# Block 0 of an attention and SwiGLU kernel: a root for each half on GpSimd, masks of the first weight pieces on VectorE, the silu table loaded first, and a written order

## The chip, the cores and the metric

The kernel runs on one core of a Trainium2 chip. The core has TensorE (matrix products and transposes, into PSUM), VectorE, ScalarE and GpSimd for elementwise work, and SyncE, which here issues nearly all DMA transfers. The engines run in parallel; each takes its own instructions in order, and semaphores make one wait for another. The metric is the device time of one execution in microseconds. A difference of 0.2% is taken here as the least that counts.

## The reference

```python
kv = np.einsum('bhsd,bhse->bhde', k, v)
out = np.einsum('bhsd,bhde->bhse', q, kv)
rms = np.sqrt(np.mean(out * out, axis=-1, keepdims=True) + 1e-06)
return (out / rms * g_norm).astype(np.float32)
...
x = np.ascontiguousarray(attn_out.transpose(0, 2, 1, 3)).reshape(B * S, H * D)
g = x @ w_gate
silu = g * (1.0 / (1.0 + np.exp(-g)))
val = x @ w_val
return (silu * val @ w_out).astype(np.float32)
```

B = 8 batches, H = 8 heads, S = 576 positions, D = 64. The 4608 tokens have 512 features; the hidden width is 1536. The inputs q, k, v and g_norm are fp32; the three weight matrices come to the chip as 64-bit words.

## The kernel before

**Tiling.** The 4608 tokens are nine blocks of 512. `Att` makes the normalised attention output x of a block, transposed so that features lie on partitions; `Ffn` multiplies it with the weights. Blocks 1 to 8 use Strassen's scheme, one or two levels deep (`Quad`, `Up`, `Inner`, `Down`, lines 544 to 940). Block 0 uses plain products (`plain_up`, lines 1026 to 1041) for the first layer, since its weights are still being prepared, and `Down` for the second.

**Weights.** Each word's high half holds the sign, the exponent and the upper bits, the low half the rest. `Words` (lines 119 to 167) turns one piece of 128x512 into fp32. `begin` takes the magnitude of the high half (ScalarE, Abs, line 146), clamps it (VectorE, line 147), masks the sign (VectorE, line 152), shifts and joins the two (VectorE, line 153). `finish` scales the low half to a unit (ScalarE, line 160) and adds it (VectorE, line 162). There are 36 pieces: w_gate and w_val in turn, 24 of them, and then 12 of w_out. `weights(n)` (line 1063) rounds pieces up to n, and keeps loading four pieces ahead (line 135, 512 KB each, on SyncE). The landing tiles come from a pool of four (`ld`), shared with k, v and q: a transfer waits until the tile's last reader is done.

**Block 0's start.** `first` (line 466): `turn_q` transposes q tiles on TensorE and copies them out of PSUM (lines 337 to 341), `first_kv` makes k'v for half of the heads (line 248), `heads` multiplies q with it (line 361). `squares` squares the products on ScalarE (line 374) and sums each head's 64 squares on VectorE (line 375). `root` takes the inverse root of both halves (256 tokens each) at once: scaling by 1/64 plus eps (line 381), a first guess by integer arithmetic (line 384), three Newton steps of three operations (lines 391 to 393), all on VectorE with tiles of 128x32. `scale` multiplies the products by it (line 113, a helper), two operations for each half; `turn_x` transposes the result on TensorE (line 410) and copies it with the gain to x on ScalarE (line 411). `warm` (line 492) runs seven products of 512 columns whose result nobody reads. Then `plain_up` (lines 1035 to 1041) multiplies x with w_gate and w_val for one of twelve slices of the hidden width, applies silu on ScalarE (line 1040) and multiplies on VectorE (line 113); slice 0 is done in halves of the tokens.

**What sets the order.** The framework orders each engine's instructions by a simulation of its own. `tc.issue_after(ins)` puts what the block traces behind `ins`, for those of its instructions that run on the engine of `ins`; it adds no wait between engines. In block 0 such lines put piece 0's `begin` behind the first half's sums and q's last copy, the second half's products behind piece 0, and the rounding of later pieces behind copies of `turn_x` (line 1094: for slice 0 behind those of the first half, from slice 1 on behind those of the second).

**Where block 0 meets block 1.** Block 1's k, v and q are loaded on SyncE behind the last weight pieces (lines 1102 to 1106). q comes in 32 small transfers (line 284) into two `ld` tiles; VectorE transposes each tile (line 331). TensorE's order in `down` (line 1002) is one product of block 0's second layer, then both halves of block 1's `heads`, then the other products.

Of the kernel before, what the change touches and what calls it, by code (L numbers as in the profile page):

```python
# [1 line left out]

# [16 lines left out]
def kernel(  # L19
# [41 lines left out]
    nc = tc.nc  # L61

    B, H, S, D = q.shape
# [7 lines left out]
    NS = DM // P  # L71
# [4 lines left out]
    eps = 1e-6  # L76
# [6 lines left out]
    consts = pool("consts", 1)  # L83
    ld_pool = pool("ld", 4)
    st_pool = pool("st", 2)
# [26 lines left out]
    sub = lambda e, o, a, b: e.tensor_tensor(out=o, in0=a, in1=b, op=OP.subtract)  # L112
    mul = lambda e, o, a, b: e.tensor_tensor(out=o, in0=a, in1=b, op=OP.mult)  # L113

    def ring():

        return r_pool.tile([P, 4, BLK], F32, name="r")

    class Words:
# [12 lines left out]
        def __init__(self, src, shape):  # L132
            self.raw = ld_pool.tile([P, LD], U32, name="ld")[:, 0 : 2 * BLK]
            dst = self.raw.rearrange("p (a b) -> p a b", a=shape[0])
            self.sent = nc.sync.dma_start(out=dst, in_=src)
            self.shape = shape
            self.begun = False

        def begin(self):

            self.begun = True
            halves = self.raw.rearrange("p (f w) -> p f w", w=2)
            low, high = halves[:, :, 0], halves[:, :, 1]
            self.low, self.room = low, ring()
            mag = self.mag = self.room[:, 1].bitcast(U32)
            nc.scalar.activation(out=mag.bitcast(F32), in_=high.bitcast(F32), func=ACT.Abs)
            nc.vector.tensor_scalar(
                out=mag.bitcast(F32), in0=mag.bitcast(F32), scalar1=self.LOW, scalar2=self.HIGH,
                op0=OP.max, op1=OP.min,
            )  # L150
            sign = self.room[:, 2].bitcast(U32)
            nc.vector.tensor_scalar(out=sign, in0=high, scalar1=0x80000000, scalar2=None, op0=OP.bitwise_and)
            return nc.vector.scalar_tensor_tensor(
                out=mag, in0=mag, scalar=3, in1=sign, op0=OP.logical_shift_left, op1=OP.bitwise_xor
            )

        def finish(self, dst):

            unit = self.room[:, 0]
            nc.scalar.activation(out=unit, in_=self.low, func=ACT.Copy, scale=2.0**-51, bias=2.0)  # L160
            a, b = self.shape[0], BLK // self.shape[0]
            return nc.vector.tensor_tensor(
                out=dst.bitcast(U32),
                in0=self.mag.rearrange("p (a b) -> p a b", a=a, b=b),
                in1=unit.bitcast(U32).rearrange("p (a b) -> p a b", a=a, b=b),
                op=OP.add,
            )
# [6 lines left out]
    words = {}  # L174
# [18 lines left out]
    class Att:  # L193
# [128 lines left out]
                for r in range(2):  # L322
                    nc.scalar.copy(out=dst[:, r], in_=self.kv_ps[r])

        def turn_q(self, i, pools=None):

            if i == 0:
                self.qt = ring().rearrange("p j (t c) -> p t j c", t=T)
            if self.quarters:
                to = self.qt[:, :, 2 * i : 2 * i + 2].rearrange("p t j c -> p j t c")  # L330
                self.q_turned = nc.vector.transpose(out=to.rearrange("p j t c -> p (j t c)"), in_=self.q[i])
                return
            for t in (2 * i, 2 * i + 1):
                pool = pools[t % 2] if pools else m_psum
                ps = pool.tile([P, NS, P], F32, name=pool.name[0])
                for j in range(NS):
                    nc.tensor.transpose(ps[:, j], self.q[t][:, j], ident)
                if t % 2 if self.n == 0 else t:
                    self.copied_q = nc.scalar.copy(out=self.qt[:, t], in_=ps)
                else:  # L340
                    nc.vector.tensor_copy(out=self.qt[:, t], in_=ps)
# [124 lines left out]
        def first(self):  # L466
            self.turn_q(0, (b_psum, c_psum))
            self.first_kv(0, (b_psum, c_psum))
            last = self.first_kv(1, (b_psum, a_psum))

            with tc.issue_after(last.ins):
                self.heads(0, (0, 1), (m_psum, m_psum))
            with tc.issue_after(self.multiplied.ins):
                self.heads(0, (2, 3))
            self.squares(0)
            with tc.issue_after(self.multiplied.ins):
                self.turn_q(1, (b_psum, c_psum))

            with tc.issue_after(self.copied_q.ins), tc.issue_after(self.summed.ins):
                begun = words[pieces[0]].begin()  # L480
            with tc.issue_after(begun.ins):
                self.product(1, (b_psum, a_psum))
            self.warm()
            self.root(0, 2)
            self.scale(0)
            with tc.issue_after(self.squared.ins), tc.issue_after(self.scaled.ins):
                weights(1)
            self.turn_x(0)
            self.scale(1)
            return self.squared, self.scaled  # L490

        def warm(self):

            ps = c_psum.tile([P, NS, P], F32, name="c")
            for _ in range(7):
                nc.tensor.matmul(ps, lhsT=ident, rhs=self.qt[:, 3], start=True, stop=True)

        def turn(self):
# [443 lines left out]
    class Ffn:  # L942
# [83 lines left out]
        def plain_up(self, f, halves=(0, 1)):  # L1026

            if 0 in halves:
                self.ps[f] = [pool.tile([P, 2, HB], F32, name=pool.name[0]) for pool in (b_psum, c_psum)]
            of = slice(halves[0], halves[-1] + 1)  # L1030
            ps = [t[:, of] for t in self.ps[f]]
            x = self.att.x[:, 0:4].rearrange("p (h m) i t -> p (m i) h t", h=2)
            for t, w in zip(ps, (wg, wv)):
                for i in range(NS):
                    nc.tensor.matmul(  # L1035
                        t, lhsT=w[f // 2][:, i, P * (f % 2) : P * (f % 2 + 1)], rhs=x[:, i, of],
                        start=(i == 0), stop=(i == NS - 1),
                    )
            h = self.h[:, f].rearrange("p (h t) -> p h t", h=2)[:, of]
            nc.scalar.activation(out=h, in_=ps[0], func=ACT.Silu)  # L1040
            mul(nc.vector, h, h, ps[1])
# [37 lines left out]
    blocks[0].load_q(1)  # L1079
    load_weights(4)  # L1080
    squared, scaled = blocks[0].first()

    for n in range(NB):
        ffn = Ffn(n, blocks[n])
        nxt = blocks[n + 1] if n + 1 < NB else None
        if n == 0:

            with tc.issue_after(squared.ins), tc.issue_after(scaled.ins):
                weights(2)
            ffn.plain_up(0, (0,))  # L1090
            copied = blocks[0].copied
            blocks[0].turn_x(1)
            for f in range(NF):
                with tc.issue_after(blocks[0].copied.ins if f else copied.ins):
                    weights(2 * (f + 2))
# [12 lines left out]
            for g in range(2):  # L1108
                nxt.kv(g)
        else:  # L1110

            def visit(g):
                with tc.issue_after(ffn.multiplied.ins):
                    nxt.kv(g)
                if nxt.n < B:
                    ffn.visited = nxt.positions

            def third():
                visit(0)
# [12 lines left out]
            ffn.up(fill)  # L1132
# [48 lines left out]
```

## Time and profile before

| | us |
|---|---|
| median of 4 runs | 1021.96 (1021.7 to 1022.2) |
| the profiled execution | 1021.87 |
| its span in the profile | 1020.0 |
| TensorE busy in the span | 1002.8 (98%) |
| VectorE busy | 702.1 (69%) |
| ScalarE busy | 228.2 (22%) |
| GpSimd busy | 370.4 (36%) |
| first x in block 0 (turn_x of the first half starts) | at 28.28 |
| from here TensorE multiplies without a wait until block 0's second layer | at 34.83 |
| last product of the plain first layer starts | at 110.49 |
| block 1's second q tile lands | at 121.02 |

Times in the profile count from the start of the span; the run's time is 1.87 us longer than the span. PE is TensorE, PEld its weight load, DVE VectorE, ACT ScalarE, POOL GpSimd, SP SyncE; a q behind the name is the engine's sequencer. In a timeline, the first number is the start, the second the duration, then come engine, line, operation, output and inputs, and the idle time before with what ended it. fp32 products show twice the number of instructions that the code has. The granted TensorE clock is 1.0 throughout.

### The profile page before, as it was taken

The numbers are of one execution on the slowest core, as the hardware profiler recorded it, in microseconds if no ns is written. First come the engines' busy times: TensorE is split into PE (matmuls) and PEld (weight loads), VectorE is DVE, ScalarE is ACT, GpSimd is POOL, SyncE is SP. The second block draws the span as 40 slices with busy tenths as digits, with TensorE's granted clock in tenths as the row PEclk, the third lists the DMA queues.
The fourth block names the chain that finished last, engine by engine and source line by source line (L and its number), as shares of the span: only waits on it lengthen the run. The fifth ranks groups of instructions, "written<-read, shape, count | busy, mean of one in ns | idle before, by whom it ended". The sixth has DMA issues, their size and how long they took to land.

```text
span 1020.0 us, 21397 instructions
## 1 busy us (share of the span) xinstructions
PE 1002.8 (98%) x8522; PEld 895.4 (88%) x8522; DVE 702.1 (69%) x1169; ACT 228.2 (22%) x353; POOL 370.4 (36%) x280
## 2 busy tenths in 40 slices
PE   5999999999999999999999999999999999999998
PEld 4544688888999999998999899988998999989997
DVE  2998788998666946685558576665669466946661
ACT  2765111221211221121121211111121211221110
POOL 0000363434055513561246315630555045513670
PEclk9999999999999999999999999999999999999999
DMA  8689643667888277846685568646872766066601
GB/s 225 198 265 258 129 92 110 183 160 163 253 221 252 53 187 204 245 89 139 207 238 135 100 208 241 170 62 193 235 202 44 179 193 191 22 168 200 194 25 42
DMA packets 273845, 170.26 MB, mean 167 GB/s; under 512 B 150609, under 2 KB 241873, under 8 KB 273745
## 3 DMA queue, kind: packets, MB, share of 16 engines
q1 hardware_dynamic: 238800, 164.42, 59.0%
q10 hardware_dynamic: 34880, 4.46, 2.7%
q8 instruction: 68, 1.11, 0.5%
q14 instruction: 33, 0.26, 0.1%
q0 software_dynamic: 64, 0.00, 0.0%
HBM read 138.02 MB, written 22.41 MB: 157 GB/s over the span
## 4 chain that ended last, share of the span: by engine, by line
PE 91%; DVE 5%; DMA 2%; issue 1%; SPq 1%; ACT 1%; DVEq 0%; ACTq 0%
PE b L728 26%; PE b L565 20%; PE c L728 13%; PE c L565 10%; PE a L728 6%; PE a L565 5%; PE b L1035 4%; PE c L1035 4%; PE m L361 1%; PE m L316 1%; DVE xi L112 1%; DMA h<-in_v_dram 1%; DVE r L112 1%; SPq L284 1%; DVE r L111 1%
## 5 line engine op out<-in xcount | busy, mean ns | idle before, releaser
L111 POOL TENSOR_TENSOR r<-r 128x256 f32<-128x256 f32 (+1 forms) x105 | 110.8, 1061 | 295.1 <-DVE r L111 292.8
L111 DVE TENSOR_TENSOR r<-b,r 128x512 f32<-128x512 f32 (+1 forms) x273 | 162.0, 606 | 64.8 <-PE b L728 60.3
L112 POOL TENSOR_TENSOR t<-wo 128x512 f32<-128x512 f32 x81 | 116.0, 1457 | 211.4 <-DVE wo L111 106.1
L111 DVE TENSOR_TENSOR r<-c,r 128x512 f32<-128x512 f32 (+1 forms) x179 | 108.5, 617 | 89.7 <-PE c L728 58.2
L728 PE MATMUL b<-x,t 128*128 128x128 f32 x1092 | 151.2, 275 | 0.0
L111 DVE TENSOR_TENSOR r<-a,r 128x512 f32<-128x512 f32 (+1 forms) x99 | 62.5, 631 | 113.0 <-PE a L565 71.1
L728 PEld LDWEIGHTS b<-x,t 128*128 128x128 f32 x1092 | 136.5, 192 | 0.8 <-DVE r L111 0.2
L728 PE MATMUL c<-xi,t 128*128 128x128 f32 x840 | 112.4, 275 | 1.0 <-DVE xi L111 1.0
L113 POOL TENSOR_TENSOR h<-r 128x1024 f32<-128x1024 f32 (+1 forms) x40 | 82.2, 2070 | 82.4 <-DVE r L111 78.8
L728 PEld LDWEIGHTS c<-xi,t 128*128 128x128 f32 x840 | 102.9, 192 | 1.2 <-DVE xi L111 1.2
L565 PE MATMUL b<-wo,h 128*128 128x256 f32 x432 | 100.1, 383 | 0.1
L565 PE MATMUL b<-t,h 128*128 128x256 f32 x432 | 96.3, 379 | 0.0
L565 PEld LDWEIGHTS b<-t,h 128*128 128x128 f32 x432 | 82.0, 190 | 11.3 <-issue 0.2
L565 PEld LDWEIGHTS b<-wo,h 128*128 128x128 f32 x432 | 79.8, 190 | 13.1 <-DVE h L113 2.5
L742 ACT COPY r<-b 128x512 f32<-128x512 f32 x63 | 36.9, 586 | 214.8 <-PE b L728 214.8
L728 PE MATMUL b<-xi,t 128*128 128x128 f32 x588 | 79.7, 276 | 0.0
L728 PEld LDWEIGHTS b<-xi,t 128*128 128x128 f32 x588 | 72.4, 192 | 0.0
L728 PE MATMUL b<-x,wg 128*128 128x128 f32 x336 | 52.8, 279 | 0.2 <-DVE x L112 0.2
L728 PE MATMUL b<-x,wv 128*128 128x128 f32 x336 | 51.2, 275 | 0.0
L565 PE MATMUL a<-wo,h 128*128 128x256 f32 x216 | 48.3, 379 | 0.0
L565 PE MATMUL c<-t,s 128*128 128x256 f32 x216 | 48.1, 379 | 0.0
L565 PE MATMUL c<-wo,h 128*128 128x256 f32 x216 | 48.1, 379 | 0.0
(133 smaller groups left out, 1562.7 us busy)
## 6 DMA issues: line engine op xcount, KB each, us to landing
t<-w SPq DMA_DIRECT2D x336, 256.0 KB, 3.5
out_dram<-r SPq DMA_DIRECT2D x17, 512.0 KB, 3.0
ld<-in_k_dram SPq DMA_DIRECT2D x26, 288.0 KB, 5.0
ld<-in_v_dram SPq DMA_DIRECT2D x26, 288.0 KB, 6.0
ld<-in_moe_w_gate_dram SPq DMA_DIRECT2D x12, 512.0 KB, 4.8
ld<-in_moe_w_val_dram SPq DMA_DIRECT2D x12, 512.0 KB, 4.7
ld<-in_moe_w_out_dram SPq DMA_DIRECT2D x12, 512.0 KB, 6.0
w<-t SPq DMA_DIRECT2D x18, 256.0 KB, 3.0
```

The lines of the kernel that those rows point to most:

```text
L111: add = lambda e, o, a, b: e.tensor_tensor(out=o, in0=a, in1=b, op=OP.add)
L112: sub = lambda e, o, a, b: e.tensor_tensor(out=o, in0=a, in1=b, op=OP.subtract)
L113: mul = lambda e, o, a, b: e.tensor_tensor(out=o, in0=a, in1=b, op=OP.mult)
L284: nc.sync.dma_start(out=to[32 * r : 32 * (r + 1), j, g0:g1], in_=q[b, 4 * i + 2 * j + h, s0 : s0 + 32 * (g1 - g0), 32 * d : 32 * (d + 1)]. ...
L316: self.positions = nc.tensor.matmul(self.kv_ps[r][u * D : (u + 1) * D, g, :], lhsT=k[:, u, c, :], rhs=v[:, u, c, :], start=(c == 0), stop= ...
L361: self.multiplied = nc.tensor.matmul(self.ps[i][u][p : p + D, t, j, :], lhsT=self.qt[rows, 2 * i + t, j, p : p + D], rhs=kvs[b % 3][rows, ...
L565: self.ffn.multiplied = nc.tensor.matmul(banks[e][:, e], lhsT=lhsT, rhs=rhs, start=first and i == 0 and (e == 0 or banks[0] is not banks[1 ...
L728: self.ffn.multiplied = nc.tensor.matmul(ps[:, i, f], lhsT=self.weight(o, p, f), rhs=self.operand(o, p), start=first and (i, f) == (0, 0), ...
L742: nc.scalar.copy(out=dst, in_=ps)
L1035: nc.tensor.matmul(t, lhsT=w[f // 2][:, i, P * (f % 2) : P * (f % 2 + 1)], rhs=x[:, i, of], start=(i == 0), stop=(i == NS - 1),)
```

## The change

Only block 0 changes, and two small tiles are made ahead of it. `power` (128x16) is filled with -0.5 on GpSimd. `early` (one column) is set to zero on VectorE, and a silu is taken of it on ScalarE, ahead of everything else in the program. `in_order` is a block that ties each instruction traced in it to the one before it on its engine, for all engines or for those named. `first` is written in one such block.

- `begin` is split in `split` (magnitude, clamp, sign), `join` (shift and xor) and `scale` (the unit). For pieces 0 and 1 `split` runs wholly on VectorE: the magnitude is a second mask in place of ScalarE's Abs.
- Piece 0's `split` comes on VectorE before the first half's sums, its `join` and `finish` before piece 1's `split` and the second half's sums.
- The q copies of the second half are both on ScalarE (one was on VectorE).
- The root is taken for each half by itself: one scaling on VectorE, then z to the power of -0.5 on GpSimd. Lines 381 to 393 are no longer used by block 0 (they are by the others).
- `warm` has four products instead of seven.
- Pieces 1 and 2 are rounded within the block too.
- On TensorE the first half of slice 0 is written ahead of `turn_x(1)`, and the rounding from piece 3 on is behind the second half's copies of `turn_x` and the second half's `scale`.

```diff
+    power = consts.tile([P, 4 * NS], F32, name="power")
+    nc.gpsimd.memset(power, -0.5)
+    early = consts.tile([P, 1], F32, name="early")
+    nc.vector.memset(early, 0.0)
+    nc.scalar.activation(out=early, in_=early, func=ACT.Silu)
...
+        for i in traced[start:]:
+            if engines and i.engine not in engines:
+                continue
+            if i.engine in before:
+                tc.add_manual_dep(
+                    i, before[i.engine].name,
+                    mybir.DependencyInfo(mybir.DependencyClass.NoSync, mybir.DependencyReason.DATA), reason="order",
+                )
+            before[i.engine] = i
...
+            if engine is nc.vector:
+                bits(sign, 0x80000000)
+                bits(mag, 0x7FFFFFFF)
+            else:
+                nc.scalar.activation(out=mag.bitcast(F32), in_=high.bitcast(F32), func=ACT.Abs)
...
-                if t % 2 if self.n == 0 else t:
+                if engine is nc.scalar or (t % 2 if self.n == 0 else t):
...
+            with in_order():
+                self.first_kv(1, (b_psum, a_psum))
                 self.heads(0, (0, 1), (m_psum, m_psum))
-            with tc.issue_after(self.multiplied.ins):
                 self.heads(0, (2, 3))
...
+                first.split(nc.vector)
+                self.square(0)
+                self.turn_q(1, (b_psum, c_psum), nc.scalar)
+                first.scale()
+                self.sum_squares(0)
+                self.inverse(0)
+                self.heads(1, range(NS), (b_psum, a_psum))
+                self.warm()
+                first.join()
+                self.square(1)
                 weights(1)
-            self.turn_x(0)
-            self.scale(1)
+                second.split(nc.vector)
+                second.scale()
+                self.sum_squares(1)
+                self.inverse(1)
+                self.scale(0)
+                self.turn_x(0)
+                second.join()
+                weights(2)
+                self.scale(1)
+                weights(3)
             return self.squared, self.scaled
...
+        def inverse(self, i):
+
+            z, y = (x[:, i].rearrange("p u t j -> p (u t j)") for x in (self.z, self.y))
+            nc.vector.tensor_scalar(out=z, in0=z, scalar1=1.0 / D, scalar2=eps, op0=OP.mult, op1=OP.add)
+            nc.gpsimd.tensor_tensor(out=y, in0=z, in1=power, op=OP.pow)
...
-            for _ in range(7):
+            for _ in range(4):
...
-            with tc.issue_after(squared.ins), tc.issue_after(scaled.ins):
-                weights(2)
-            ffn.plain_up(0, (0,))
-            copied = blocks[0].copied
-            blocks[0].turn_x(1)
+            with in_order(ffn_engine):
+                ffn.plain_up(0, (0,))
+                blocks[0].turn_x(1)
             for f in range(NF):
-                with tc.issue_after(blocks[0].copied.ins if f else copied.ins):
+                with tc.issue_after(blocks[0].copied.ins), tc.issue_after(scaled.ins):
                     weights(2 * (f + 2))
```

More of the change, by code (lines that the diff above doesn't have):

```diff
@@ L1 @@
-from contextlib import ExitStack
+from contextlib import ExitStack, contextmanager
 import concourse.bass as bass
@@ L113, with in_order @@
     mul = lambda e, o, a, b: e.tensor_tensor(out=o, in0=a, in1=b, op=OP.mult)
+    power = consts.tile([P, 4 * NS], F32, name="power")
[3 more added lines that the diff above has]
+    nc.scalar.activation(out=early, in_=early, func=ACT.Silu)
+    @contextmanager
+    def in_order(*engines):
+        traced = nc.cur_bb.bb.instructions
+        last = traced[-1]
+        yield
+        start = next(k for k in reversed(range(len(traced))) if traced[k] is last) + 1
+        before = {}
+        for i in traced[start:]:
[7 more added lines that the diff above has]
+            before[i.engine] = i
     def ring():
@@ L136, in __init__, with split @@
             self.shape = shape
-            self.begun = False
+            self.begun = self.scaled = False
         def begin(self):
             self.begun = True
+            self.split()
+            return self.join()
+        def split(self, engine=None):
             halves = self.raw.rearrange("p (f w) -> p f w", w=2)
             low, high = halves[:, :, 0], halves[:, :, 1]
-            self.low, self.room = low, ring()
+            self.low, self.high, self.room = low, high, ring()
             mag = self.mag = self.room[:, 1].bitcast(U32)
-            nc.scalar.activation(out=mag.bitcast(F32), in_=high.bitcast(F32), func=ACT.Abs)
+            sign = self.room[:, 2].bitcast(U32)
+            bits = lambda to, mask: nc.vector.tensor_scalar(
+                out=to, in0=high, scalar1=mask, scalar2=None, op0=OP.bitwise_and
+            )
+            if engine is nc.vector:
[3 more added lines that the diff above has]
+                nc.scalar.activation(out=mag.bitcast(F32), in_=high.bitcast(F32), func=ACT.Abs)
             nc.vector.tensor_scalar(
@@ L150, in begin, with join @@
             )
-            sign = self.room[:, 2].bitcast(U32)
-            nc.vector.tensor_scalar(out=sign, in0=high, scalar1=0x80000000, scalar2=None, op0=OP.bitwise_and)
+            if engine is not nc.vector:
+                bits(sign, 0x80000000)
+        def join(self):
+            self.begun = True
+            mag, sign = (self.room[:, i].bitcast(U32) for i in (1, 2))
             return nc.vector.scalar_tensor_tensor(
@@ L155, in begin, with scale @@
             )
+        def scale(self):
+            self.scaled = True
+            nc.scalar.activation(out=self.room[:, 0], in_=self.low, func=ACT.Copy, scale=2.0**-51, bias=2.0)
         def finish(self, dst):
+            if not self.scaled:
+                self.scale()
             unit = self.room[:, 0]
-            nc.scalar.activation(out=unit, in_=self.low, func=ACT.Copy, scale=2.0**-51, bias=2.0)
             a, b = self.shape[0], BLK // self.shape[0]
@@ L323, in kv, with turn_q @@
                     nc.scalar.copy(out=dst[:, r], in_=self.kv_ps[r])
-        def turn_q(self, i, pools=None):
+        def turn_q(self, i, pools=None, engine=None):
             if i == 0:
@@ L468, in first @@
             self.first_kv(0, (b_psum, c_psum))
-            last = self.first_kv(1, (b_psum, a_psum))
-            with tc.issue_after(last.ins):
+            first, second = words[pieces[0]], words[pieces[1]]
+            self.z, self.y = (st_pool.tile([P, 2, 2, 2, NS], F32, name=x) for x in "zy")
+            self.sq = ring().rearrange("p f (t j d) -> p f t j d", t=2, j=NS)
+            with in_order():
+                self.first_kv(1, (b_psum, a_psum))
                 self.heads(0, (0, 1), (m_psum, m_psum))
-            with tc.issue_after(self.multiplied.ins):
@@ L474, in first @@
                 self.heads(0, (2, 3))
[L475 to L486, printed above, removed]
-                weights(1)
@@ new lines, in first, with square @@
+                second.split(nc.vector)
[8 more added lines that the diff above has]
+                weights(3)
+            return self.squared, self.scaled
+        def square(self, i):
+            for u in range(2):
+                self.squared = nc.scalar.activation(out=self.sq[:, 2 * i + u], in_=self.ps[i][u], func=ACT.Square)
@@ new lines, in sum_squares @@
+        def sum_squares(self, i):
+            for u in range(2):
+                nc.vector.tensor_reduce(
+                    out=self.z[:, i, u], in_=self.sq[:, 2 * i + u], axis=mybir.AxisListType.X, op=OP.add
+                )
+        def inverse(self, i):
+            z, y = (x[:, i].rearrange("p u t j -> p (u t j)") for x in (self.z, self.y))
+            nc.vector.tensor_scalar(out=z, in0=z, scalar1=1.0 / D, scalar2=eps, op0=OP.mult, op1=OP.add)
+            nc.gpsimd.tensor_tensor(out=y, in0=z, in1=power, op=OP.pow)
@@ L1034, in plain_up @@
                 for i in range(NS):
[L1035 removed]
+                    self.multiplied = nc.tensor.matmul(
                         t, lhsT=w[f // 2][:, i, P * (f % 2) : P * (f % 2 + 1)], rhs=x[:, i, of],
@@ L1081 @@
     squared, scaled = blocks[0].first()
+    ffn_engine = blocks[0].multiplied.ins.engine
     for n in range(NB):
```

## The prediction

> **What bounds the kernel now.** The page comes first: TensorE is busy for 1002.8 of 1020.0 us, so only time in which it waits, or does filler work, can be won. The change touches block 0 alone, so I read VectorE's timeline there (start, duration, operation):
>
> ```profile
> 18.76 0.69 DVE L341 COPY r<-b 128x512 f32<-128x512 f32 x1 [1.62 <-PE b L337]
> 19.37 1.27 DVE L375 TENSOR_REDUCE z<-r 128x8 f32<-128x512 f32 x2
> 21.67 0.43 DVE L147 TENSOR_SCALAR r<-r 128x512 f32<-128x512 f32 x1 [1.03 <-ACT r L146]
> ...
> 23.07 1.27 DVE L375 TENSOR_REDUCE z<-r 128x8 f32<-128x512 f32 x2
> 24.38 0.18 DVE L381 TENSOR_SCALAR z<-z 128x32 f32<-128x32 f32 x1
> ...
> 26.62 0.19 DVE L393 SCALAR_TENSOR_TENSOR y<-a,y 128x32 f32<-128x32 f32 x1
> 26.84 1.29 DVE L113 TENSOR_TENSOR r<-m,y 128x512 f32<-128x512 f32 x2
> ```
>
> Sums, eleven small operations for the root, then scaling: all of it stands before TensorE's next useful work, and TensorE spends that time on the filler of line 496 (21.73 to 28.0). The chain of waits goes on:
>
> ```profile
> 28.28 0.64 PE m L410 x4
> 28.94 0.46 ACT x L411
> ...
> 31.95 1.28 ACT L1040
> ...
> 34.83 0.48 PE b L1035
> ```
>
> From 28.28 TensorE is nearly full: its own waits to 34.83 are 0.34 and 0.20 us, as the second half's transposes slip in ahead of wv's half. After 34.83 it waits for nothing up to 110. VectorE, which rounds the weights, is as full in that stretch (columns: PE, PEld, DVE, ACT, POOL busy):
>
> ```profile
> 34.83:110.00 75.17, 75.17 (x183) 34.88 (x184) 71.47 (x143) 45.23 (x76) 1.08 (x1) 1.00 0.84 241
> ```
>
> Last, the chain where block 0 meets block 1, and SyncE's waits there:
>
> ```profile
> 119.07 1.92 DMA ld<-in_q_dram
> ...
> 121.12 1.26 DVE r L331
> ...
> 122.42 0.27 PE m L361
> ```
> ```profile
> SPq L284 <- DVE r L152: 1.2, 1, 1.2
> ```
>
> Block 1's q comes in 32 transfers that SyncE issues one after the other from 100.24 (when the mask of a w_out piece, line 152, frees the tile) to 119.5; the last lands at 121.02, is transposed by 122.37, and TensorE takes it at 122.42, just as its first product (to 122.4) is done. So this second chain has only about 0.05 us of slack: TensorE can't profit from being earlier than the weight stream is.
>
> **What the Trainium skill says.** "ScalarE: Activation LUTs" (What ACT_TABLE_LOAD costs) gives 1283 ns; the trace has 1.28 us twice. The drain that the page adds is not seen: silu starts at 33.24, where the load ends. "TensorE: Matmul & The Clock Gate" (What's actually happening) has the clock fall after an idle window of about 3.4 us; here four transposes take 1.09 us at 4.17 and 0.66 us at 18.07, and the 1.05 us gap at 18.7 slows nothing. "SBUF — State Buffer" (SBUF: two separate sides) says that GpSimd and a VectorE operation with two SBUF inputs or in a 2-port mode exclude each other for a whole instruction. The trace agrees:
>
> ```profile
> 137.19 1.55 POOL L112 TENSOR_TENSOR t<-wv 128x512 f32<-128x512 f32 x1 [1.33 <-DVE wv L111]
> 138.70 3.39 POOL L112 TENSOR_TENSOR t<-wg,wv 128x512 f32<-128x512 f32 x2
> ```
> ```profile
> 137.53 1.75 DVE L112 TENSOR_TENSOR wv<-wv 128x512 f32<-128x512 f32 x1
> ...
> 154.77 0.68 DVE L112 TENSOR_TENSOR wv<-wv 128x512 f32<-128x512 f32 x1
> ```
>
> The same subtraction takes 0.68 us alone and 1.75 us beside GpSimd.
>
> **The change, part by part.** Times are those of the profiled execution.
>
> First half. TensorE's order up to 21.80 stays, with the 1.05 us gap (nothing in the profile explains it; I keep it). Piece 0 (issued 11.14, landing 6.4 us later) is there at 17.54. VectorE: sign 17.6, magnitude 17.94, clamp to 18.81 (0.42 each, 0.34 apart), idle time before. The q copy of 0.69 us goes to ScalarE, so the sums run 18.83 to 20.1, the scaling by 1/64 plus eps to 20.32, the xor (0.69) to 20.97. Then the rounding's last addition waits for ScalarE's unit: squares to 19.27, q copies to 19.8 and 21.06, unit 20.95 to 21.63. Addition at 21.67.
>
> GpSimd's power (128x16) isn't in the trace. Below: its two-input rows,
>
> ```profile
> L111 POOL TENSOR_TENSOR r<-r 128x256 f32<-128x256 f32 x84 | 61.2, 736 | 239.8 <-DVE r L111 238.7 <-DMA t<-w 0.9
> L111 POOL TENSOR_TENSOR r<-r 128x1024 f32<-128x1024 f32 x21 | 49.6, 2361 | 55.3 <-DVE r L111 54.1 <-POOL t L112 1.2
> ```
>
> give 2.1 ns a column and 0.19 us fixed, so 0.22 us for 16 columns at an add's price. Value taken, an estimate: "GPSIMD Engine Reference" (Performance pitfalls for Q7 kernels) has 4 cycles for each dependent fp32 step; some 20 such steps (my guess for a logarithm and an exponential) at 1.2 GHz are 67 ns a column, 1.07 us, with the fixed part 1.25 us. Above: three or four times the steps, 4 us. It can't begin before the xor ends at 20.97 (two SBUF inputs), ends at 22.22, and holds the addition of 21.67 back by 0.55 us.
>
> Second half. Addition 22.22 to 22.9, mask and clamp of piece 1 from 22.8 (1.1 us more work ahead of the sums), sums at 23.93 (their squares are ready at 22.94), one scaling at 25.24, scale(0) from 25.45. Before it was 26.84: of the root's 2.46 us (24.38 to 26.84) 0.2 stays, 0.31 goes because the sums start later, 0.55 to the lock. Gain 1.39. The second power hides: scale(0) needs only the first half's root, reads one SBUF input, and scale(1) comes at 28.1, 2.6 us later. Seven fillers become four: 21.8 to 25.3, then 1.6 us idle, too little for the clock.
>
> TensorE: turn_x(0) at 26.89, wg's half at 28.29 (1.40 later, as before), wv's at 30.12 (piece 1 is done at 28.1), turn_x(1) at 31.95, next half at 33.35, against 34.83: 1.48 earlier. The second half's transposes no longer fill the wait for wv, but it has no wait either.
>
> Early table: 1.28 us out of ScalarE's stretch after 28, and into its start. If it stands ahead of ScalarE's four k and v transfers (0.74 to 3.6), they go 1.3 to 1.8 us later; the last lands at 11.3 and is needed after 14.28, so it is covered by 3 us. The two small memsets fall into idle time of VectorE and GpSimd.
>
> Weight stream. Pieces from 3 on now queue on ScalarE behind turn_x(1)'s copies (before, two pieces stood behind turn_x(0)'s). Copies at 32.61 and to 33.88, Abs of piece 3 to 34.45, then clamp 0.45, xor 0.60, addition 0.60: piece 4 begins at 36.1 on VectorE instead of 36.49. The masks and the product that came earlier (three times 0.33 and 0.34 us) fit into VectorE's idle 31.5 to 34.45. With the wait of 0.2 us at 37.12 gone, the stream is 0.6 us ahead, not 1.5. SyncE's pieces 4 and 5 go out earlier (21.7 and 24 instead of 23.5 and 30.7), but VectorE, not the transfers, sets the pace until 85. From there everything queues behind it: w_out pieces, block 1's k and v, its q.
>
> So TensorE waits at block 1's second product, and keeps 0.6 + 0.05 us: 1021.87 - 0.65 = 1021.2 us. The profiled execution stands 0.09 below the median of 1021.96, so this is about 0.75 under the median.
>
> **Rivals.** *The stream follows.* If the power costs under 0.7 us, or the scheduler packs more of the rounding into VectorE's idle time, or the gap of 1.05 us goes, the q chain moves by 1.6 to 2.9 us: 1019.0 to 1020.3. For it: VectorE has 2.9 us idle there to be filled; against: the copies that gate ScalarE. *A slow power* ends on the other side. Beyond 0.7 us each us of it delays the addition, and through it sums, scaling, stream and q chain one for one; from about 3 us the second power holds piece 1 back too, and TensorE's idle time after its filler (1.1 us and the hold) passes 3.4 us, so its clock may fall. Taking 1.3 us as the undelayed stream's lead, 2 us are lost when the hold is 3.3 us, so from a power of 4 us or slightly less; at 5 us the time is about 1025. For it: no row shows this operation; against: only 16 columns. *Nothing is left.* The second order of q, the lock and a differently packed VectorE eat the 0.6 us: 1021.5 to 1022.5. For it: the q chain's slack of 0.05 us makes every 0.1 us of the stream count.
>
> **How the numbers follow.** Forecast 0.48, stream follows 0.22, slow power 0.17, nothing left 0.13. A difference under 0.2% (2.04 us) is what a measurement can't tell from none. Most of the second case (0.17) passes it, all of the third, none of the others: faster 0.17, same 0.66, slower 0.17. The range 1019.5 to 1024.5 leaves out the ends of the two outer cases, some 0.07 and 0.12.
>
> **What would show it.** Power near 1.25 us at 21, with the addition behind it; scale(0) near 25.5; turn_x(0) near 26.9; line 1035's second half near 33.4; one table load; and, decisive, a wait of about 0.9 us of TensorE before block 1's second product at 121. Wrong if that wait is missing, if the power takes over 3 us, or if q's first transfer starts over 1.5 us before 100.24.

## The result, and the profile after

The changed kernel takes 1023.57 us (median, 1021.83 to 1024.76, 33 runs), the kernel before 1021.91 (1020.17 to 1023.62, 53 runs): a ratio of 1.0016, 95% interval 1.0011 to 1.0021, so 1.66 us slower where 0.65 faster was forecast. The profiled execution took 1023.26 us with a span of 1021.5.

VectorE's timeline of the changed kernel first (start, duration, operation; L560 the scaling ahead of the root, L210 the rounding's last addition):

```profile
19.04 0.18 DVE L560 TENSOR_SCALAR z<-z 128x16 f32<-128x16 f32 x1
...
19.95 0.69 DVE L210 CUSTOM_DVE_ANT_0 wg<-r 128x1024 uint16<-128x1024 uint16 x1
...
23.08 1.28 DVE L113 TENSOR_TENSOR r<-m,y 128x512 f32<-128x512 f32 x2
...
26.19 0.69 DVE L113 TENSOR_TENSOR r<-b,y 128x512 f32<-128x512 f32 x1 [0.39 <-POOL y L561]
...
29.22 0.69 DVE L210 CUSTOM_DVE_ANT_0 wg<-r 128x1024 uint16<-128x1024 uint16 x1
35.03 0.42 DVE L113 TENSOR_TENSOR h<-h,c 128x256 f32<-128x256 f32 x1 [5.12 <-PE c L1106]
```

The first scaling starts at 23.08, where it stood at 26.84. Yet from 29.9 to 35.03 VectorE has nothing to do. TensorE's timeline says why (L458 `turn_x`, L1106 slice 0 of the plain first layer):

```profile
24.42 1.09 PE L458 MATMUL m<-ident,r 128*128 128x128 f32 x8 [0.90 <-DVE r L113]
25.86 0.70 PE L1106 MATMUL b<-x,wg 128*128 128x256 f32 x2 [0.34 <-ACT x L459]
29.96 2.40 PE L1106 MATMUL b<-x,wg 128*128 128x256 f32 x6 [3.41 <-DVE wg L210]
32.16 2.79 PE L1106 MATMUL c<-x,wv 128*128 128x256 f32 x8
34.78 1.04 PE L458 MATMUL m<-ident,r 128*128 128x128 f32 x8
36.16 1.99 PE L1106 MATMUL b<-x,wg 128*128 128x256 f32 x8 [0.34 <-ACT x L459]
```

`turn_x` of the first half is 3.86 us earlier than before (28.28). Then wg's half runs one of its four steps and waits 3.41 us for the addition of 29.22. That addition is *piece 2*, the wg weights of slice 1, which slice 0 doesn't need; its own piece 0 was finished at 20.64. Slices 0 and 1 share one tile of wg. After the wait the same products run at a lower granted clock (columns: sum, then PE, PEld, DVE, ACT, POOL busy, then clock, DMA share, GB/s):

```profile
30.00:35.00 5.00, 5.00 (x17) 4.05 (x18) 0.00 (x0) 0.38 (x1) 0.00 (x0) 0.66 0.22 77
36.16:111.33 75.17, 75.17 (x183) 34.87 (x184) 71.59 (x143) 46.54 (x78) 1.49 (x2) 1.00 0.82 240
```

So the second half of slice 0 starts at 36.16 where it started at 34.83, and from there TensorE is as full as before. The chain where block 0 meets block 1 moved along with it:

```profile
120.85 1.93 DMA ld<-in_q_dram
...
122.91 1.26 DVE r L379
...
124.21 0.27 PE m L409
```

124.21 stood at 122.42. Two more lines belong to the result, GpSimd's power for each half:

```profile
19.37 3.23 POOL L561 TENSOR_TENSOR y<-z,power 128x16 f32<-128x16 f32 x1 [16.34 <-DVE z L560]
23.25 2.90 POOL L561 TENSOR_TENSOR y<-z,power 128x16 f32<-128x16 f32 x1 [0.65 <-DVE z L560]
```

### The profile page after: what moved, and what is told of

It reads as the page before. It is cut to its first block, busy times and chain, and to the rows that moved or that the text cites. A ratio compares the mean times of both kernels' runs of the same rounds, so it can differ in the third digit from the quotient of the medians.

```text
span 1021.5 us, 21379 instructions
## 1 busy us (share of the span) xinstructions
PE 1001.7 (98%) x8516; PEld 895.6 (88%) x8516; DVE 701.0 (69%) x1162; ACT 226.5 (22%) x352; POOL 376.1 (37%) x283
## 3 DMA queue, kind: packets, MB, share of 16 engines
q1 hardware_dynamic: 238800, 164.42, 57.2%
## 4 chain that ended last, share of the span: by engine, by line
PE 84%; DVE 11%; DMA 3%; SPq 1%; issue 1%; ACT 0%; POOL 0%; DVEq 0%; ACTq 0%
PE b L799 26%; PE b L636 20%; PE c L799 13%; PE c L636 10%; PE a L799 6%; PE a L636 5%; DVE r L195 2%; PE m L409 1%; PE m L364 1%; SPq L332 1%; DVE r L112 1%; DVE xi L112 1%; DVE r L184 1%; DVE r L176 1%; DMA h<-in_v_dram 1%
## 5 line engine op out<-in xcount | busy, mean ns | idle before, releaser
L111 DVE TENSOR_TENSOR r<-c,r 128x512 f32<-128x512 f32 (+1 forms) x179 | 108.5, 617 | 90.4 <-PE c L799 58.6
L1106 PE MATMUL b<-x,wg 128*128 128x512 f32 (+1 forms) x104 | 44.8, 571 | 4.1 <-DVE wg L210 3.4
```

The source lines that it names most:

```text
L111: add = lambda e, o, a, b: e.tensor_tensor(out=o, in0=a, in1=b, op=OP.add)
L1106: self.multiplied = nc.tensor.matmul(t, lhsT=w[f // 2][:, i, P * (f % 2) : P * (f % 2 + 1)], rhs=x[:, i, of], start=(i == 0), stop=(i == N ...
```

## The experiments

Three explanations stood at first. A: the wait comes from the order in which the pieces are written down, piece 2 ahead of slice 0's products into the tile that they read. B: GpSimd's power holds the others up. C: a second chain, from the rounding stream to block 1's q, limits what a better start can bring. A fourth, D, came from a view that none of the three explains.

### Piece 2 behind, or in another tile

`third_behind` writes piece 2's rounding behind slice 0's first products:

```diff
                 self.scale(1)
-                weights(3)
...
                 ffn.plain_up(0, (0,))
+                weights(3)
                 blocks[0].turn_x(1)
```

> The changed kernel with one thing moved: the rounding of piece 2 is traced behind the first half of slice 0 instead of ahead of it; the engines' own order stays. Theory A (a wait that the trace order makes: piece 2 fills the other half of the weight tile that slice 0 reads, and TensorE waits for it as if it were its own): the wait of 3.4 us for wg is gone, slice 0's second half starts 5 us earlier than in the changed kernel, the rounding stream some 3 us earlier, and the time is about 1.0 us under the kernel before, 1020.9 us. Theory B (GpSimd's power of 3 us is what holds VectorE and so TensorE): the wait stays and the time is that of the changed kernel, 1023.5 us.

Measured: 1017.71 us, ratio 0.996 (0.9948 to 0.9973).

`other_tile` keeps piece 2 ahead, but rounds slice 2, which lies in another tile, before slice 1:

```diff
-    pieces = [(x, j) for j in range(NF) for x in "gv"] + [("o", j) for j in range(NF)]
+    slices = [0, 2, 1] + list(range(3, NF))
+    pieces = [(x, j) for j in slices for x in "gv"] + [("o", j) for j in range(NF)]
...
-            for f in range(NF):
+            for at, f in enumerate(slices):
...
-                    weights(2 * (f + 2))
+                    weights(2 * (at + 2))
```

> The changed kernel with its order as it is, but the third piece to be rounded is one of another weight tile (slices 0, 2, 1, 3 and on, instead of 0, 1, 2, 3). Theory A: no wait for wg, as the tile that slice 0 reads is complete with piece 0; time about 1020.9 us, within 0.5 us of the kernel that moves the rounding. Theory B: the wait and 1023.5 us stay.

Measured: 1017.21 us, ratio 0.9956 (0.9944 to 0.9969), the fastest median of all, and faster than both kernels. Its TensorE timeline:

```profile
23.66 1.09 PE L458 MATMUL m<-ident,r 128*128 128x128 f32 x8 [0.71 <-DVE r L113]
25.10 1.99 PE L1106 MATMUL b<-x,wg 128*128 128x256 f32 x8 [0.34 <-ACT x L459]
...
30.03 1.99 PE L1106 MATMUL b<-x,wg 128*128 128x256 f32 x8 [0.34 <-ACT x L459]
```

All eight products in one go. From `turn_x` to the second half it is 6.37 us here and 11.74 in the changed kernel: 5.37 us, of which 3.41 are the wait and the other 1.96 mostly the lower clock (0.66 over 5 us is 1.7 us of work lost). The power stands in this kernel unchanged (3.23 and 2.90 us), so B isn't the cause, but for 0.4 us of the wait (below). The second half starts 5.2 us (third_behind) and 6.1 us (other_tile) earlier than in the changed kernel, where I expected 5. Yet both kernels came out over 3 us under the 1020.9 that I expected; the section on addresses shows what was missing. A holds: the same piece, rounded as early, costs nothing in another tile. Why one step passed: piece 2 fills columns 128 to 255 of each of the tile's four rows, slice 0 reads columns 0 to 127. No element is shared, but the write's span runs from the first row's middle to the last row's end. Slice 0's first step reads ahead of that span, its other three inside it, and exactly those three waited; that the framework compares spans is my inference from this.

The kernel before has piece 2 behind. `before_third_ahead` moves it there:

```diff
             with tc.issue_after(squared.ins), tc.issue_after(scaled.ins):
-                weights(2)
+                weights(3)
             ffn.plain_up(0, (0,))
```

> The kernel before with the suspected cause alone: piece 2 is rounded ahead of slice 0's first half in the program too (three pieces instead of two). Theory A: TensorE waits about 4 us for wg with its first product begun, its clock falls, and the time rises by 3 to 5 us to 1025 to 1027 us. Theory B: no wait, 1021.9 us.

Measured: 1025.12 us, ratio 1.0032 (1.002 to 1.0044). The size is as expected, the form not quite: without an order written down the second half's transposes moved in, the rest of wg's half went behind wv's, and the long wait became that of the second half's wg for the first half's silu, which came late (TensorE's timeline):

```profile
29.67 0.70 PE L1035 MATMUL b<-x,wg 128*128 128x256 f32 x2 [0.34 <-ACT x L411]
30.20 1.04 PE L410 MATMUL m<-ident,r 128*128 128x128 f32 x8
...
39.10 2.44 PE L1035 MATMUL b<-x,wg 128*128 128x256 f32 x8 [2.44 <-ACT h L1040]
```

### The gate of the rounding stream

`third_behind_gate` and `other_tile_gate` release slice 1's rounding after the first half's copies again, as in the kernel before:

```diff
                 ffn.plain_up(0, (0,))
+                copied = blocks[0].copied
...
-                with tc.issue_after(blocks[0].copied.ins), tc.issue_after(scaled.ins):
+                with tc.issue_after(blocks[0].copied.ins if f else copied.ins), tc.issue_after(scaled.ins):
```

> As the kernel that moves piece 2's rounding, and the rounding from piece 3 on is put behind the first half's copies of turn_x again, as it was before the change. Theory C (the second chain, rounding stream to block 1's q, sets what the front can win): the stream and q's first transfer come another 2 us earlier, and the time falls by 1 to 2 us more, to 1019.0 to 1020.0 us. If the stream is not what limits, the time is that of the kernel without this, 1020.9 us.

> The changed kernel with slices 0, 2, 1, and its rounding stream of slice 1 released by the first half's copies instead of the second's, as in the kernel before. Theory C (with the first slice 3.8 us sooner, the end is set by block 1's q, whose transfers are issued behind the stream; 0.75 us of wait was seen): time 0.5 to 1 below other_tile's 1017.21, the wait for VectorE's q transpose gone. Rival (the gate's place is nothing, as my forecast's 0.6 us at most): 1017.2 within 0.3.

Measured: 1017.32 us, 0.9956 (0.9944 to 0.9969), against 1017.71 without the gate; and 1017.54 us, 0.9955 (0.9943 to 0.9967), against 1017.21. The gate's place makes no difference that these runs can tell. In other_tile's profile TensorE waits 0.75 us for block 1's q, with the gate it doesn't; but in that execution block 0's start was 0.9 us later too, so the wait's absence proves little. So these runs don't show C.

### The addresses

One thing in the changed kernel's profile had no place in any step: the second half's keys and values are added up at 15.49 on VectorE, before at 16.85, and nothing ahead of them was changed but an early silu and two small memsets. Before, then changed:

```profile
16.85 0.29 DVE L111 TENSOR_TENSOR kv<-a,kv 128x128 f32<-128x128 f32 x1 [2.64 <-PE a L248]
```
```profile
15.49 0.29 DVE L111 TENSOR_TENSOR kv<-a,kv 128x128 f32<-128x128 f32 x1 [2.14 <-PE a L296]
```

In the table of queues (packets, MB, share of 16 engines' time) the same transfers take less time. Before, then changed:

```profile
q1 hardware_dynamic: 238800, 164.42, 59.0%
```
```profile
q1 hardware_dynamic: 238800, 164.42, 57.2%
```

The two new constants take 96 bytes of each partition, and all tiles behind them move up. Theory D: before, the tiles into which transfers land start 32 bytes above a multiple of 64 (`ld` at 93856); with 96 more they start at multiples of 128, and transfers are faster. Three kernels move the addresses alone, by a tile that is written once and never read:

```diff
     wo = consts.tile([P, NF, DM], F32, name="wo")
+    pad = consts.tile([P, 24], F32, name="pad")
+    nc.gpsimd.memset(pad, 0.0)
```

That is `before_shift96`; `[P, 8]` in its place makes `before_shift32`, and the same 32 bytes in the changed kernel and in other_tile make `after_shift32` and `other_tile_shift32`, whose targets are then 32 above a multiple of 128, as before. `before_early` has the early silu alone, with no address moved:

```diff
+    early = st_pool.tile([P, 2, 2, 2, NS], F32, name="a")[:, 0, 0, 0, 0:1]
+    nc.vector.memset(early, 0.0)
+    nc.scalar.activation(out=early, in_=early, func=ACT.Silu)
```

> The kernel before with one 96-byte constant tile per partition more (zeroed once by GpSimd, never read), so that every later tile, those into which transfers land among them, moves up by 96 bytes: from addresses that are 32 above a multiple of 64 to multiples of 128, which is where the two new constants of the change put them. No step of the computation differs. Theory D (addresses): transfers land sooner, the second half's keys and values near 13.0 us instead of 14.31, and the time falls by at least those 1.3 us, to 1019 to 1020.7. Its rival (the change's order or the early table makes them land sooner, and addresses do nothing): second half's keys and values at 14.3, time within 0.5 us of the kernel before.

> The changed kernel with one 32-byte constant tile more, which puts the tiles behind it back to 32 above a multiple of 64, all else as changed. Theory D: the transfers land as late as in the kernel before (keys and values of the second half near 14.3) and the changed kernel takes 1024.5 to 1026, since its 1023.57 would hide a gain that isn't in the list of its edits. Rival: as the changed kernel, 1023 to 1024.

> The changed kernel with the weight slices rounded in the order 0, 2, 1, so that the piece written ahead lies in another tile, and with the 32-byte constant more. Theory D: 1018.5 to 1020, 1.3 to 2.5 above the same kernel at multiples of 128 bytes (1017.21). Rival: 1017.2 within 0.4. What it stays below the kernel before, at the same addresses, is then what the listed edits bring once the wait for the weight tile is gone: some 2 to 3 us under Theory D.

> The kernel before with a 32-byte constant tile more, so that the targets of transfers start at odd multiples of 64 bytes. The 96-byte shift (multiples of 128) gave 1019.75 against 1022.24. Theory D64 (a multiple of 64 is enough): within 0.5 us of 1019.75. Theory D128 (only multiples of 128 help): as the kernel before, 1021.9 to 1022.5. A rival to both, that another 32-byte tile alone changes nothing and the 96-byte result came by another way than addresses, gives the second number too.

> The kernel before with the early silu of one element alone, its scratch taken from a tile that is there already, so that no address of a transfer's target moves (all stay 32 above a multiple of 64). My step: the load of 1.28 us that stands in the kernel before at 31.95 goes to the start of ScalarE's line, nothing in block 0's start waits for it longer than 0.2 us, and the time moves by 0 to -0.5 us. Rival: an early load also lets transfers start sooner or later by ScalarE's issues (keys and values are issued from ScalarE's queue): time off by over 1 us either way.

Measured (ratios to runs of the kernel before made beside them):

| | targets modulo 128 | us | ratio, 95% interval |
|---|---|---|---|
| before_shift32 | 64 | 1021.85 | 0.9999 (0.9991 to 1.0007) |
| before_shift96 | 0 | 1019.75 | 0.998 (0.9972 to 0.9987) |
| changed | 0 | 1023.57 | 1.0016 (1.0011 to 1.0021) |
| after_shift32 | 32 | 1026.69 | 1.0047 (1.0035 to 1.006) |
| other_tile | 0 | 1017.21 | 0.9956 (0.9944 to 0.9969) |
| other_tile_shift32 | 32 | 1020.98 | 0.9994 (0.9984 to 1.0005) |
| before_early | 32 | 1021.71 | 0.9997 (0.9989 to 1.0005) |

In all three pairs the addresses at multiples of 128 are worth 2.0 to 3.9 us by the ratios, and an odd multiple of 64 is worth nothing. All the moved tiles that start at a multiple of 128 here start at one of 256 too (`ld` at 93952), so these runs don't tell the two apart. Two of my ranges were missed: after_shift32 (1024.5 to 1026) and other_tile_shift32 (1018.5 to 1020) are both slower, since the addresses were worth more than I thought and the edits less, 0.6 us instead of 2 to 3. The queue's share of other_tile_shift32 and of before_shift96 goes the same way:

```profile
q1 hardware_dynamic: 238800, 164.42, 59.5%
```
```profile
q1 hardware_dynamic: 238800, 164.42, 57.8%
```

Over all fourteen profiles the share is 57.2 to 58.3% in the eight kernels at multiples of 128 and 58.6 to 59.5% in the six others. That transfers land sooner shows best in ScalarE's first transfer of keys, issued at 0.75 us and the first on its queue: it takes 3.35 to 3.46 us from issue to landing in the eight, 3.86 to 4.01 in the six.

For the second half's keys and values I expected TensorE to start on them at 13.0 in before_shift96 and at 14.3 in after_shift32; it did at 13.90 and 13.59, so a single profile doesn't separate the two there. Their addition on VectorE varies by over a microsecond between profiles at the same addresses (14.89 to 16.25 us in the eight, 16.13 to 16.96 in the six). D is shown by the medians and by the first transfer; which of the moved tiles matters, and why, wasn't tried. The early silu alone changes nothing measurable.

### What the power is worth

`other_tile_steps` takes each half's root in the ten small VectorE steps of the kernel before:

```diff
             nc.vector.tensor_scalar(out=z, in0=z, scalar1=1.0 / D, scalar2=eps, op0=OP.mult, op1=OP.add)
-            nc.gpsimd.tensor_tensor(out=y, in0=z, in1=power, op=OP.pow)
+            a = st_pool.tile([P, 2, 2, 2, NS], F32, name="a")[:, i].rearrange("p u t j -> p (u t j)")
+            nc.vector.tensor_scalar(
+                out=y.bitcast(I32), in0=z.bitcast(I32), scalar1=-0.5, scalar2=float(0x5F3759DF),
+                op0=OP.mult, op1=OP.add,
+            )
+            for _ in range(3):
+                nc.vector.scalar_tensor_tensor(out=a, in0=y, scalar=-0.5, in1=y, op0=OP.mult, op1=OP.mult)
+                nc.vector.tensor_tensor(out=a, in0=a, in1=z, op=OP.mult)
+                nc.vector.scalar_tensor_tensor(out=y, in0=a, scalar=1.5, in1=y, op0=OP.add, op1=OP.mult)
```

> The changed kernel with slices 0, 2, 1 (1017.21) and each half's root in the ten small VectorE steps of the kernel before, in place of GpSimd's power; all else the same. Prices the power. If VectorE's own order sets the start (two roots of about 10 x 0.22 = 2.2 us each on it): the first transposes of half 0 about 2 us later, the second half of the first slice about 3 later, time 1019 to 1021. If the power's 3.2 and 2.9 us held things up as much as VectorE's steps would (Theory B): no later, 1016.5 to 1017.6.

Measured: 1024.86 us, ratio 1.0029 (1.0019 to 1.0039), so 7.6 us above other_tile, twice the most that I expected. Its TensorE timeline:

```profile
28.98 1.97 PE L458 MATMUL m<-ident,r 128*128 128x128 f32 x8 [5.00 <-DVE r L113]
30.87 3.44 PE L1114 MATMUL b<-x,wg 128*128 128x256 f32 x8
...
37.26 1.99 PE L1114 MATMUL b<-x,wg 128*128 128x256 f32 x8 [0.34 <-ACT x L459]
```

I had counted one root ahead of the first scaling. In the order written down both stand ahead of it (the second half's root at 25.67 to 27.7, the scaling at 27.65): 4 us, and 1.3 that this execution's keys and values came later, make the 5.3 us of `turn_x` (VectorE's timeline):

```profile
25.67 0.17 DVE L562 TENSOR_SCALAR y<-z 128x16 int32<-128x16 int32 x1
...
27.65 1.28 DVE L113 TENSOR_TENSOR r<-m,y 128x512 f32<-128x512 f32 x2
```

Then the transposes and wg's half take 1.97 and 3.44 us instead of 1.09 and 1.99. The power itself isn't cheaper: it takes 3.23 us where the ten steps take about 2.1. What it brings is that VectorE goes on beside it.

`other_tile_steps_warm` fills that wait with 14 instead of 4 filler products:

```diff
-            for _ in range(4):
+            for _ in range(14):
                 nc.tensor.matmul(ps, lhsT=ident, rhs=self.qt[:, 3], start=True, stop=True)
```

> The kernel with slices 0, 2, 1 and the root in VectorE's small steps (1024.86; TensorE waits 5.0 us for the first scaled half and its granted clock over 26 to 36 us is 0.66), with 14 instead of 4 filling products of TensorE ahead of that wait, which fill about 4.6 of the 5.0 us. Theory: a wait of TensorE costs its length and then some 2 to 2.5 us of lower clock, which also follows the changed kernel's 3.4 us wait. Then filling brings back only the second part: 1022.3 to 1023, the clock over 26 to 36 at 1.0, the first transposes at the same time. Rival (the lower clock costs nothing at the end, or the filling does not keep it): 1024.5 to 1025.5.

Measured: 1026.36 us, ratio 1.0045 (1.0031 to 1.0059). My own sizing failed: a filler product is two instructions of 0.43 us, so ten more took 8.6 us (12.28 against 3.70), not 4.6, and ran past the scaling. The stretch 26 to 36 of both kernels, without and with them, and the later one's timeline, still tell what the clock costs:

```profile
26.00:36.00 10.00, 7.02 (x26) 5.85 (x27) 7.53 (x20) 2.87 (x5) 0.00 (x0) 0.66 0.24 80
```
```profile
26.00:36.00 10.00, 9.66 (x36) 5.95 (x35) 6.54 (x14) 2.79 (x5) 0.00 (x0) 1.00 0.04 6
```
```profile
31.34 1.04 PE L458 MATMUL m<-ident,r 128*128 128x128 f32 x8
...
37.66 1.99 PE L1114 MATMUL b<-x,wg 128*128 128x256 f32 x8 [0.34 <-ACT x L459]
```

It starts the transposes 2.36 us later (31.34 against 28.98) and the second half only 0.40 later: at the full clock the stretch between is 1.96 us shorter, as much as the changed kernel lost after its wait. This pair doesn't show it as a time at the end, since the median rose by 1.5. The single runs of before_third_ahead point to it: the three with a mean granted clock of 1.0 took 1024.1 to 1024.8 us, the three with 0.998 took 1025.4 to 1026.9.

### Where all of it is decided

| profiled execution | k and v added | `turn_x` | second half of slice 0 | span | span less second half |
|---|---|---|---|---|---|
| before | 16.85 | 28.28 | 34.83 | 1020.0 | 985.2 |
| before_shift96 | 15.86 | 27.27 | 33.83 | 1018.6 | 984.8 |
| changed | 15.49 | 24.42 | 36.16 | 1021.5 | 985.3 |
| after_shift32 | 16.13 | 25.97 | 39.00 | 1024.9 | 985.9 |
| other_tile | 14.91 | 23.66 | 30.03 | 1015.8 | 985.8 |
| other_tile_shift32 | 16.45 | 26.01 | 32.37 | 1018.6 | 986.2 |
| other_tile_steps | 16.25 | 28.98 | 37.26 | 1023.3 | 986.0 |

From the second half of slice 0 on, each of these takes 984.8 to 986.2 us, and the start varies by nine: the start decides. Some of the 1.4 us between them is a wait for block 1's q, which is 1.0 us in other_tile_shift32 and missing in before and before_shift96.

## Why the prediction was wrong

The result is a sum of two things that my steps did not have. The ratios at like addresses give it: the listed edits cost 1.0047 less 1, that is 4.8 us (3.6 to 6.1), as after_shift32 shows, and the addresses give 3.2 of it back (1.0047 less 1.0016).

**"wg's half at 28.29 (1.40 later, as before)": the step that failed.** I had only asked whether piece 0 was done. The written order puts piece 2's addition into the same tile ahead of these products, and they wait for it: 3.41 us, and 1.96 of lower clock after it. At the addresses of the kernel before, the second half comes 6.6 us earlier with this wait removed (TensorE's timelines of after_shift32, with it, and other_tile_shift32, without):

```profile
25.97 1.09 PE L460 MATMUL m<-ident,r 128*128 128x128 f32 x8 [0.71 <-DVE r L115]
...
31.52 2.93 PE L1108 MATMUL b<-x,wg 128*128 128x256 f32 x6 [3.41 <-DVE wg L212]
...
39.00 1.99 PE L1108 MATMUL b<-x,wg 128*128 128x256 f32 x8 [0.34 <-ACT x L461]
```
```profile
26.01 1.09 PE L460 MATMUL m<-ident,r 128*128 128x128 f32 x8 [0.70 <-DVE r L115]
...
32.37 1.99 PE L1108 MATMUL b<-x,wg 128*128 128x256 f32 x8 [0.34 <-ACT x L461]
```

The wait is again 3.41 us, but what follows it loses 3.3 us, not 1.96: the lower clock lasted longer there (0.66 over 30 to 40 us). Part of the 3.2 us between the changed kernel and after_shift32 may be this. No rival of mine named it; the slow-power rival ended on the right side by a wrong mechanism.

**The power.** Estimated 1.25 us, 4 at the most; measured 3.23 and 2.90. The sequel was wrong as well: I had the power and VectorE exclude each other, from the Trainium skill, "SBUF — State Buffer" (SBUF: two separate sides), and rows of the kernel before that agree with it. Here L210's addition, with two SBUF inputs, ran at 19.95 in the middle of the power for its usual 0.69 us. The measurement decides: no 0.55 us of lock. The second power held the second half's scaling up by 0.39 us. In the changed kernel VectorE goes on from there with hardly a pause to the addition of 29.22, so about 0.4 of TensorE's 3.41 us come from it; in other_tile, where the hold is 0.40, TensorE has no such wait. So the point "over 3 us" at which I called myself wrong was passed, with little harm.

**scale(0) at 25.45, turn_x at 26.89.** With the lock left out my sum gives 1.94 us of gain instead of 1.39. At the addresses of the kernel before, other_tile_shift32 has `turn_x` at 26.01, 2.27 earlier. The addition that I had at 21.67 starts at 21.54 there, so 0.13 of it is an earlier start, and 2.14 stand against 1.94. But for the lock, the arithmetic of that half was right to 0.2 us.

**The gap of 1.05 us** between q's transposes, which I kept: it is missing in the changed kernel (16.98 and 17.59) and there again in after_shift32 (1.5 us, put down to issue), other_tile_shift32 (1.4) and before_shift96 (1.3). Its cause stays open.

**Early table, memsets.** Costed at nothing: before_early moves by -0.3 us (-1.1 to 0.5) by its ratio. Right, and cheaper than thought: the four k and v transfers that ScalarE issues were to go 1.3 to 1.8 us later, but the table loads beside them and the last starts at 2.98 us, before at 2.97.

**The second chain.** I had q follow 0.9 us less than TensorE's start, and named the wait before block 1's second product the decisive sign. Where the wait for the weight tile is gone and the addresses are those of before, it is there, with the size forecast, 0.9 (TensorE's waits in other_tile_shift32):

```profile
PE m L411 <- DVE r L381: 1.0, 1, 1.0
```

The start gains 2.46 us there, q's last landing (119.44 against 121.02) 1.58: 0.88 apart. That this matches is in part luck, for both terms are 1 us above mine (1.48 and 0.6). q's first transfer starts at 98.41, 1.83 before 100.24, which is past my sign of 1.5 and within the rival of the stream that follows (1.6 to 2.9). The kernel gains 0.6 us by its ratio (0.5 slower to 1.6 faster): the forecast of 0.65 lies in that interval, and so does no gain. The wait depends on the order of the rounding too: third_behind, with the second half at 31.01, has none. In the changed kernel itself q's first transfer starts at 101.92, later than before, and the same line says 0.5.

So the sign was wrong by one unseen wait. That the time stayed within 0.2%, and inside the range, is owed to the addresses, which no step had.

## What to carry to other kernels

When a write is moved ahead of a read, look at everything else in the same tile: a piece that the reader doesn't use can hold it, if the write's span crosses what is read. Give what is loaded ahead a tile of its own. And before a small change is judged, look whether it moved the addresses of the transfers' targets: here a 96-byte tile that nobody reads was worth 2.0 us in the kernel before, more than the 0.6 that the edits bring once the wait is gone.

## What was not expected of the hardware

- Transfers into tiles whose start moved from 32 modulo 128 bytes to a multiple of 128 (here also of 256): the first transfer of keys landed after 3.35 to 3.46 us instead of 3.86 to 4.01, the main queue's share of time fell from 59.0 to 57.8% for the same packets, and the kernel by 0.2% (0.13 to 0.28). Odd multiples of 64: 59.5%, no gain.
- GpSimd's power of 128x16 takes 2.90 to 3.26 us, 180 to 200 ns a column, and a VectorE addition with two SBUF inputs isn't slowed beside it (0.69 us at 19.95).
- With waits of 3.4 and 5.0 us TensorE's granted clock was 0.66 in the stretches (5 and 10 us) that hold what followed, the second with the end of the wait, and the work there took about 2 us longer; in after_shift32, after the same wait of 3.4 us, it was 0.66 over 30 to 40 us, and 3.3 us were lost. These waits agree with the 3.4 us that the prediction took from the Trainium skill, "TensorE: Matmul & The Clock Gate" (What's actually happening). But the 2.44 us of before_third_ahead are shorter, and there too the clock was 0.67 over 39.10 to 44.34.
